# A SwiGLU feed-forward on one core: the head of the kernel, with half of the first row block transposed by DMA and its gate computed slice by slice of D

## The chip, the core and the metric

The kernel runs on one core of a Trainium2 chip. The core has a matrix engine (TensorE, PE in the profile, with its weight loads listed apart as PEld), VectorE (DVE), ScalarE (ACT), GpSimd (POOL) and SyncE (SP), which here only issues DMAs. Matmuls read SBUF and write PSUM. DMAs move data between HBM and SBUF; one kind (DMA_TRANSPOSE, the crossbar copy) transposes on its way. The metric is the device time of the whole program in microseconds, the median of several runs, with one launch. A profile is one execution; its span runs from the first instruction to the last.

## The reference

With x of 2048 rows and D = 640 columns and F = 1536 features, all in bf16:

```python
B, S, D, F = 1, 2048, 640, 1536

def reference(x, w_gate, w_up, w_down):
    g = _silu(x @ w_gate)
    u = x @ w_up
    return (g * u) @ w_down
```

## The kernel before

**Tiling.** Rows are cut into four blocks of 512 (`S_BLK`), D into five slices of 128 (`KD`, index `kd`), F into twelve chunks of 128 (`KF`, index `fc`). For each row block and each feature chunk, `proj` runs five matmuls (one for each slice of D) into a PSUM tile `pg` (gate), and five into `pu` (up). A weight block 128x128 is the stationary operand, and the transposed x, `xT`, is the moving one, with 512 columns, one for each row of x. `gate` then has ScalarE compute silu(pg) into SBUF (`sg`) and VectorE multiply it with `pu` into `aT`, in bf16. When a row block has its twelve chunks, the down projection multiplies `aT` with `w_down`: columns 512 to 639 of the output first, transposed (`po_t`), then four times 128 rows by 512 columns (`po_a`). The last four rows of x have their gate and up values from dot products on VectorE (`row_dots`), in gaps of its work; that part isn't touched.

**How x becomes xT.** Two ways are used. TensorE transposes a 128x128 block by a matmul with the identity (`transpose_chunk`, tile `pt` in PSUM), and ScalarE or VectorE copies the result into `xT`; this serves the first row block, whose x lies in `x_sb`. The other three row blocks come through `turn_x`, a crossbar copy by DMA issued on SyncE's queue: that of block 1 behind the weight loads, those of blocks 2 and 3 after the first row block.

**The head.** The first row block starts while its data is still arriving. `load_x` brings chunks of 128 rows: 0, 1 and 3 on SyncE, 2 on ScalarE. The weights come in pieces that grow (`W_CHUNKS`: feature chunks 0; 1; 2-3; 4-7; 8-11, gate then up); the first is split over both queues. `head()` writes TensorE's order out: 18 filler matmuls on a tile of ones (`warm`), which compute nothing that is used; the transposes of chunks 0 and 2, two fillers, those of chunk 1, two fillers; the projections of feature chunks 0 and 1 on rows 0 to 383; in between the transposes of chunk 3; then the remaining 128 rows. Feature chunks 2 to 11 follow in the loop at full width, in each of them five matmuls for gate and then five for up.

**What sets the order.** `keep_order` fixes the traced order on TensorE, ScalarE, VectorE and SyncE. ScalarE's queue holds its DMA issues, then the load of its function table and a first silu on one column (`silu_first`), then the copies of `xT`. Every DMA gets one of eight completion semaphores, in turn over both queues; a DMA whose semaphore is still in use by an earlier one waits on its issuing engine until that one has landed. In PSUM, gate and up tiles share the tag `gu` with four buffers, and the filler target `pw` takes one of them at the start; `po_a` and `po_b` have two each, and the transposes use them in the head.

Of the kernel before, what the change touches and what calls it, by code (L numbers as in the profile page):

```python
# [10 lines left out]
def _body(  # L11
# [8 lines left out]
    nc = tc.nc  # L20
    P = nc.NUM_PARTITIONS
    f32 = mybir.dt.float32
    bf16 = mybir.dt.bfloat16
    ACT = mybir.ActivationFunctionType
# [10 lines left out]
    S_BLK = 512  # L35
    NSB = S // S_BLK
    SUB = S_BLK // P
    DA = 512
    Q = 32
    N_WARM, N_GAP = 18, 2  # L40
    T = 4
    WT_STEP = 4
    ROW_J = 0
    W_CHUNKS = [(0, 1), (1, 2), (2, 4), (4, 8), (8, 12)]
    assert D % P == 0 and F % P == 0 and S % S_BLK == 0 and D > DA and SUB == 4

    consts = ctx.enter_context(tc.tile_pool(name="consts", bufs=1))
# [4 lines left out]
    )  # L52

    ident = consts.tile([P, P], bf16)
    x_sb = consts.tile([P, SUB, D], bf16)
    xT = consts.tile([P, KD, S], bf16)
    wg_sb = consts.tile([P, KD, F], bf16)
    wu_sb = consts.tile([P, KD, F], bf16)
# [18 lines left out]
    def wslice(a, b):  # L77
        return slice(a * P, b * P)

    def load_w(eng, dst, src, a, b):  # L80
        eng.dma_start(out=dst[:, :, wslice(a, b)], in_=src[:, :, wslice(a, b)])

    def load_x(eng, c0, c1):
        eng.dma_start(out=x_sb[:, c0:c1, :], in_=x_v[:, c0:c1, :])
# [14 lines left out]
        for a, b in zip(traced, traced[1:]):  # L99
            issue_order(a, b)  # L100

    ones = consts.tile([P, P], bf16)
    silu_first = consts.tile([P, 1], f32)
    nc.vector.memset(ones[:], 1.0)  # L104

    load_x(nc.sync, 0, 1)
    load_x(nc.scalar, 2, 3)
    load_x(nc.sync, 1, 2)
    for dst, src, k in ((wg_sb, wg_v, 3), (wu_sb, wu_v, 2)):
        for eng, k0, k1 in ((nc.scalar, 0, k), (nc.sync, k, KD)):  # L110
            eng.dma_start(out=dst[:, k0:k1, wslice(0, 1)], in_=src[:, k0:k1, wslice(0, 1)])
    load_w(nc.sync, wg_sb, wg_v, *W_CHUNKS[1])
    load_x(nc.sync, 3, 4)
    nc.scalar.activation(silu_first[:], ones[:, 0:1], ACT.Silu)
    load_w(nc.sync, wu_sb, wu_v, *W_CHUNKS[1])
    for a, b in W_CHUNKS[2:]:
        load_w(nc.sync, wg_sb, wg_v, a, b)
        load_w(nc.sync, wu_sb, wu_v, a, b)
    nc.sync.dma_start(out=wd_sb[:], in_=wd_v)
    wgt_v = w_gate.rearrange("d (kf p) -> d kf p", p=P)  # L120
    wut_v = w_up.rearrange("d (kf p) -> d kf p", p=P)

    def turn_x(sb):
        s_sl = slice(sb * S_BLK, (sb + 1) * S_BLK)
        nc.sync.dma_start_transpose(out=xT[:, :, s_sl], in_=xt_v[s_sl])

    def turn_w(dst, src):
        for a in range(0, KF, WT_STEP):
# [1 line left out]
                out=dst[:, a : a + WT_STEP, :], in_=src[:, a : a + WT_STEP, :]  # L130
            )

    turn_x(1)
    nc.sync.dma_start(
        out=x_row[:],
        in_=x2[S - T : S, :].rearrange("t d -> (t d)").partition_broadcast(P),
# [29 lines left out]
    def do_dots(n):  # L166
        for _ in range(n):
            next(dots, None)

    pw = psum.tile([P, S_BLK], f32, tag="gu", name="pw", bufs=4)  # L170

    def warm(n):
        for _ in range(n):
            nc.tensor.matmul(  # L174
                pw[:, 0:P], lhsT=ones[:], rhs=ones[:], start=True, stop=True
            )

    def transpose_chunk(c, parts):
# [8 lines left out]
                )  # L187
            copy(out=xT[:, k0:k1, c_sl], in_=pt[:])  # L188

    def proj(ps, w_sb, fc, sb, c0, c1, cols=lambda ap: ap):  # L190
        for kd in range(KD):
            nc.tensor.matmul(  # L192
                cols(ps[:, c0:c1]),
                lhsT=w_sb[:, kd, fc * P : (fc + 1) * P],
                rhs=cols(xT[:, kd, sb * S_BLK + c0 : sb * S_BLK + c1]),
                start=(kd == 0),
                stop=(kd == KD - 1),
            )

    def outer_chunks(ap):  # L200
        return ap.rearrange("p (c r) -> p c r", r=P)[:, 0:3:2]

    def gu_tiles():
        pg = psum.tile([P, S_BLK], f32, tag="gu", name="pg", bufs=4)
        pu = psum.tile([P, S_BLK], f32, tag="gu", name="pu", bufs=4)
        return pg, pu
# [8 lines left out]
        )  # L215

    def head():

        dve, act = nc.vector.tensor_copy, nc.scalar.copy
        split = [(act, "po_a", 0, 2), (dve, "po_b", 2, KD)]
        late = (SUB - 1) * P
        (pg0, pu0), (pg1, pu1) = gu_tiles(), gu_tiles()
        warm(N_WARM)
        transpose_chunk(0, [(dve, "po_a", 0, KD)])
        transpose_chunk(2, [(dve, "po_b", 0, KD)])
        warm(N_GAP)  # L230
        transpose_chunk(1, split)
        warm(N_GAP)
        proj(pg0, wg_sb, 0, 0, 0, late, outer_chunks)
        proj(pg0, wg_sb, 0, 0, P, 2 * P)
        proj(pu0, wu_sb, 0, 0, 0, late)
        proj(pg1, wg_sb, 1, 0, 0, late)
        transpose_chunk(3, split)
        proj(pu1, wu_sb, 1, 0, 0, late)
        for fc, pg, pu in ((0, pg0, pu0), (1, pg1, pu1)):
            proj(pg, wg_sb, fc, 0, late, S_BLK)  # L240
            proj(pu, wu_sb, fc, 0, late, S_BLK)
            gate(pg, pu, 0, fc, S_BLK)
        keep_order(mybir.EngineType.PE)
        keep_order(mybir.EngineType.Activation)

    head()
    for sb in range(NSB):
        n_s = S_BLK if sb < NSB - 1 else S_BLK - T
        for fc in range(KF):
            if sb == 0 and fc < 2:  # L250
                continue
            pg, pu = gu_tiles()
            proj(pg, wg_sb, fc, sb, 0, n_s)
            proj(pu, wu_sb, fc, sb, 0, n_s)
            gate(pg, pu, sb, fc, n_s)
            if sb > 0 and fc < KF - 2:
                do_dots(2)
# [51 lines left out]
                    row_tail()  # L309
                eng.dma_start(out=out2[s0 : s0 + P, c0:c1], in_=ot[:])  # L310
        if sb == 0:
            turn_x(2)
            turn_w(wuT, wut_v)
            turn_x(3)
    keep_order(mybir.EngineType.DVE)
    keep_order(mybir.EngineType.SP)

# [104 lines left out]
```

## Time and profile before

| what | value |
|---|---|
| time, median of 3 runs | 163.86 us (163.79 to 163.90) |
| the profiled execution's own time (its span) | 162.06 us |
| TensorE busy | 159.1 us, 98% of the span, 799 matmuls |
| VectorE / ScalarE busy | 111.7 / 42.8 us |
| gate and up matmuls, busy | 59.5 / 59.9 us |
| down projection matmuls, busy | 42.5 + 10.3 us |
| HBM read / written | 7.21 / 2.62 MB |

The span leaves out what lies around the first and the last instruction; it is 1.8 us under the median time. In the timeline a row is a run of like instructions: start, length, engine, line, operation, output and inputs, count, and in brackets the idle time before it and what ended it. "SPq" and "ACTq" rows are the issues of DMAs on SyncE and ScalarE; the length of an issue is the time that the engine spends on it, and "to landing" is counted from the start of the issue until the data has arrived. Busy times of matmuls are unions of overlapping instructions, so the pace of a stretch is read from the distance between starts.

### The profile page before, as it was taken

Reading aid. Unit: us, or ns where it says so; the run is one execution under the profiler, and the core shown is the slowest. Engines: PE = TensorE matmul, PEld = TensorE weight load, DVE = VectorE, ACT = ScalarE, POOL = GpSimd, SP = SyncE. Lnnn points to the kernel's source line nnn. Section 1 sums busy time; section 2 is a strip of 40 time slices with the busy share of each in tenths; the row PEclk is TensorE's granted clock in tenths of the full one; section 3 lists DMA queues with packets and bytes.
Section 4 is the critical chain, followed back from the end, with each engine's and each line's share of the span. In section 5 each row is a group of like instructions: output and inputs, shape, how many; then the busy total and the mean of one; then the engine's idle time right before and its main releaser. Section 6 shows DMA issues by size and latency. Waiting matters only on the chain.

```text
span 162.1 us, 2137 instructions
## 1 busy us (share of the span) xinstructions
PE 159.1 (98%) x799; PEld 77.5 (48%) x811; DVE 111.7 (69%) x251; ACT 42.8 (26%) x74; POOL 0.6 (0%) x6
## 2 busy tenths in 40 slices
PE   9999999999999999999999999999999999999995
PEld 8754444444444444444444444444444444445454
DVE  2242223599469999979919999979964999993000
ACT  3142222112222222221222322221214222222121
POOL 1000000000000000000000000000000000000000
DMA  7999999999089990003110000000320000000312
GB/s 211 252 316 366 360 210 263 230 229 94 32 191 177 241 226 12 0 0 34 65 65 0 4 0 2 0 0 3 62 69 32 0 0 0 0 4 0 51 38 73
DMA packets 42729, 15.86 MB, mean 98 GB/s; under 512 B 34528, under 2 KB 42592, under 8 KB 42720
## 3 DMA queue, kind: packets, MB, share of 16 engines
q1 hardware_dynamic: 33824, 14.88, 37.0%
q10 hardware_dynamic: 8896, 0.85, 5.5%
q8 instruction: 6, 0.10, 0.3%
q14 instruction: 3, 0.02, 0.0%
HBM read 7.21 MB, written 2.62 MB: 61 GB/s over the span
## 4 chain that ended last, share of the span: by engine, by line
PE 98%; issue 1%; DVE 0%
PE pu L192 32%; PE pg L192 32%; PE po_a L292 26%; PE po_t L263 6%; PE pw L174 1%; PE pt L183 1%; DVE ot_b L304 0%; DVE ones L104 0%
## 5 line engine op out<-in xcount | busy, mean ns | idle before, releaser
L192 PE MATMUL pg<-xT,wg_sb 128*128 128x512 bf16 (+4 forms) x248 | 59.5, 366 | 0.4
L192 PE MATMUL pu<-xT,wu_sb 128*128 128x512 bf16 (+3 forms) x250 | 59.9, 370 | 0.0
L213 DVE TENSOR_TENSOR aT<-sg,pu 128x512 bf16<-128x512 f32 (+1 forms) x48 | 32.7, 683 | 29.3 <-PE pu L192 27.9
L212 ACT ACTIVATE sg<-pg 128x512 f32<-128x512 f32 (+1 forms) x48 | 28.6, 596 | 67.4 <-PE pg L192 64.3
L292 PE MATMUL po_a<-wd_sb,aT 128*128 128x512 bf16 (+2 forms) x212 | 42.5, 358 | 0.2
L145 DVE SCALAR_TENSOR_TENSOR prod<-wgT,x_row 128x640 f32<-128x640 bf16 x48 | 39.4, 821 | 1.1
L145 DVE SCALAR_TENSOR_TENSOR prod<-wuT,x_row 128x640 f32<-128x640 bf16 x48 | 39.4, 821 | 1.0
L192 PEld LDWEIGHTS <-wg_sb 128*128 128x128 bf16 x255 | 24.3, 98 | 27.5 <-DMA wg_sb<-in_w_gate_dram 0.3
L192 PEld LDWEIGHTS <-wu_sb 128*128 128x128 bf16 x250 | 24.0, 98 | 27.5 <-DMA wu_sb<-in_w_up_dram 0.2
L292 PEld LDWEIGHTS <-aT 128*128 128x128 bf16 x216 | 20.7, 98 | 21.7 <-issue 0.2
L301 ACT CAST ot<-po_a 128x512 bf16<-128x512 f32 (+1 forms) x17 | 9.5, 561 | 32.1 <-PE po_a L292 19.9
L263 PE MATMUL po_t<-aT,wd_sb 128*128 128x512 bf16 (+1 forms) x47 | 10.3, 365 | 0.1
L263 PEld LDWEIGHTS <-wd_sb 128*128 128x128 bf16 x48 | 4.7, 98 | 5.1
L304 DVE CAST ot_b<-po_a 128x128 bf16<-128x128 f32 x1 | 0.3, 291 | 9.9 <-PE po_a L292 9.9
L188 DVE COPY xT<-pt 128x640 bf16<-128x640 bf16 (+1 forms) x4 | 1.7, 424 | 5.5 <-PE pt L183 5.5
L272 ACT CAST ot_t<-po_t 128x512 bf16<-128x512 f32 (+1 forms) x4 | 2.2, 559 | 11.6 <-PE po_t L263 11.6
L145 DVE DVE_READ_ACCUMULATOR prod<-wuT,x_row 128x1 f32 x48 | 3.9, 82 | 0.0
L145 DVE DVE_READ_ACCUMULATOR prod<-wgT,x_row 128x1 f32 x48 | 3.9, 81 | 0.0
L274 DVE STREAM_TRANSPOSE ot_q<-ot_t 128x512 bf16<-128x512 bf16 (+1 forms) x4 | 2.7, 676 | 1.7 <-ACT ot_t L272 1.7
L174 PE MATMUL pw<-ones 128*128 128x128 bf16 x22 | 2.8, 304 | 0.4 <-DVE ones L104 0.4
L174 PEld LDWEIGHTS <-ones 128*128 128x128 bf16 x22 | 2.3, 143 | 0.4 <-DVE ones L104 0.4
L183 PE MATMUL pt<-ident,x_sb 128*128 128x128 bf16 x20 | 2.2, 270 | 0.0
(13 smaller groups left out, 5.5 us busy)
## 6 DMA issues: line engine op xcount, KB each, us to landing
wd_sb<-in_w_down_dram SPq DMA_DIRECT2D x1, 1920.0 KB, 13.9
out_dram<-ot SPq DMA_DIRECT2D x15, 128.0 KB, 1.7
wg_sb<-in_w_gate_dram SPq DMA_DIRECT2D x2, 640.0 KB, 7.7
wu_sb<-in_w_up_dram SPq DMA_DIRECT2D x2, 640.0 KB, 8.6
x_row<-in_x_dram SPq DMA_DIRECT2D x1, 640.0 KB, 4.7
x_sb<-in_x_dram SPq DMA_DIRECT2D x3, 160.0 KB, 3.0
out_dram<-ot_q ACTq DMA_DIRECT2D x12, 32.0 KB, 1.9
wg_sb<-in_w_gate_dram SPq DMA_DIRECT2D x1, 320.0 KB, 4.8
```

Of the source, the lines that this page charges most:

```text
L145: nc.vector.scalar_tensor_tensor(out=prod[:], in0=wT[:, fc, :], scalar=1.0, in1=x_row[:, t, :], op0=ALU.mult, op1=ALU.mult, accum_out=acc[ ...
L174: nc.tensor.matmul(pw[:, 0:P], lhsT=ones[:], rhs=ones[:], start=True, stop=True)
L183: nc.tensor.transpose(out=pt[:, kd - k0, :], in_=x_sb[:, c, kd * P : (kd + 1) * P], identity=ident[:],)
L188: copy(out=xT[:, k0:k1, c_sl], in_=pt[:])
L192: nc.tensor.matmul(cols(ps[:, c0:c1]), lhsT=w_sb[:, kd, fc * P : (fc + 1) * P], rhs=cols(xT[:, kd, sb * S_BLK + c0 : sb * S_BLK + c1]), st ...
L212: nc.scalar.activation(sg[:, 0:n_s], pg[:, 0:n_s], ACT.Silu)
L213: nc.vector.tensor_tensor(out=aT[:, fc, s0 : s0 + n_s], in0=sg[:, 0:n_s], in1=pu[:, 0:n_s], op=ALU.mult)
L263: nc.tensor.matmul(po_t[:], lhsT=wd_sb[:, kf, DA:D], rhs=aT[:, kf, sb * S_BLK : sb * S_BLK + n_t], start=(kf == 0), stop=(kf == KF - 1),)
L272: nc.scalar.copy(ot_t[:], po_t[:])
L274: nc.vector.transpose(out=ot_q[:], in_=ot_t[:])
L292: nc.tensor.matmul(po[:], lhsT=aT[:, kf, s0 : s0 + P], rhs=wd_sb[:, kf, c0:c1], start=(kf == 0), stop=(kf == KF - 1),)
L301: nc.scalar.copy(ot[:], po[:])
```

## The change

The first row block is made from two halves. Rows 0-255 still come into `x_sb` and are transposed by TensorE, but each chunk of 128 rows is now loaded by columns: columns 0-255 on SyncE, 256-639 on ScalarE, which are also the two parts of its copy into `xT`. Rows 256-511 come by a crossbar copy, straight into `xT`. The gate weights of feature chunks 0-3 come as five slices of D, alternating between the queues; the up weights of these chunks follow behind the crossbar copy in two pieces.

`head()` holds four gate tiles at once (`EARLY`), goes over the slices of D in the outer loop and over the four feature chunks in the inner one, for rows 0-255 first (slice 0 in two steps of 128 rows) and for rows 256-511 then. After that come the up projections of the four chunks at full width, in the tiles `po_a` and `po_b`. The fillers are 16, all at the start, and both of their operands are one column of ones read 128 times over.

The moves on the queues: ScalarE issues four DMAs ahead of its table load (two pieces of x, gate slices 1 and 3) where it issued three; SyncE issues two pieces of x, gate slices 0, 2 and 4, the crossbar copy, and then the up weights.

```diff
--- before.py
+++ after.py
@@ -35,13 +35,15 @@
     S_BLK = 512
     NSB = S // S_BLK
     SUB = S_BLK // P
+    HALF = S_BLK // 2
     DA = 512
     Q = 32
-    N_WARM, N_GAP = 18, 2
+    N_WARM = 16
     T = 4
     WT_STEP = 4
     ROW_J = 0
-    W_CHUNKS = [(0, 1), (1, 2), (2, 4), (4, 8), (8, 12)]
+    EARLY = 4
+    W_CHUNKS = [(4, 8), (8, 12)]
     assert D % P == 0 and F % P == 0 and S % S_BLK == 0 and D > DA and SUB == 4
 
     consts = ctx.enter_context(tc.tile_pool(name="consts", bufs=1))
@@ -52,7 +54,7 @@
     )
 
     ident = consts.tile([P, P], bf16)
-    x_sb = consts.tile([P, SUB, D], bf16)
+    x_sb = consts.tile([P, HALF // P, D], bf16)
     xT = consts.tile([P, KD, S], bf16)
     wg_sb = consts.tile([P, KD, F], bf16)
     wu_sb = consts.tile([P, KD, F], bf16)
@@ -99,38 +101,40 @@
         for a, b in zip(traced, traced[1:]):
             issue_order(a, b)
 
-    ones = consts.tile([P, P], bf16)
+    def turn_x(r0, r1):
+        nc.sync.dma_start_transpose(out=xT[:, :, r0:r1], in_=xt_v[r0:r1])
+
+    ones = consts.tile([P, 1], bf16)
     silu_first = consts.tile([P, 1], f32)
     nc.vector.memset(ones[:], 1.0)
 
-    load_x(nc.sync, 0, 1)
-    load_x(nc.scalar, 2, 3)
-    load_x(nc.sync, 1, 2)
-    for dst, src, k in ((wg_sb, wg_v, 3), (wu_sb, wu_v, 2)):
-        for eng, k0, k1 in ((nc.scalar, 0, k), (nc.sync, k, KD)):
-            eng.dma_start(out=dst[:, k0:k1, wslice(0, 1)], in_=src[:, k0:k1, wslice(0, 1)])
-    load_w(nc.sync, wg_sb, wg_v, *W_CHUNKS[1])
-    load_x(nc.sync, 3, 4)
-    nc.scalar.activation(silu_first[:], ones[:, 0:1], ACT.Silu)
-    load_w(nc.sync, wu_sb, wu_v, *W_CHUNKS[1])
-    for a, b in W_CHUNKS[2:]:
+    for c in range(HALF // P):
+        for eng, k0, k1 in ((nc.sync, 0, 2), (nc.scalar, 2, KD)):
+            d_sl = slice(k0 * P, k1 * P)
+            eng.dma_start(out=x_sb[:, c, d_sl], in_=x_v[:, c, d_sl])
+    for kd in range(KD):
+        eng = (nc.sync, nc.scalar)[kd % 2]
+        eng.dma_start(
+            out=wg_sb[:, kd, wslice(0, EARLY)], in_=wg_v[:, kd, wslice(0, EARLY)]
+        )
+    turn_x(HALF, S_BLK)
+    nc.scalar.activation(silu_first[:], ones[:], ACT.Silu)
+    for a in range(0, EARLY, 2):
+        load_w(nc.sync, wu_sb, wu_v, a, a + 2)
+    for a, b in W_CHUNKS:
         load_w(nc.sync, wg_sb, wg_v, a, b)
         load_w(nc.sync, wu_sb, wu_v, a, b)
     nc.sync.dma_start(out=wd_sb[:], in_=wd_v)
     wgt_v = w_gate.rearrange("d (kf p) -> d kf p", p=P)
     wut_v = w_up.rearrange("d (kf p) -> d kf p", p=P)
 
-    def turn_x(sb):
-        s_sl = slice(sb * S_BLK, (sb + 1) * S_BLK)
-        nc.sync.dma_start_transpose(out=xT[:, :, s_sl], in_=xt_v[s_sl])
-
     def turn_w(dst, src):
         for a in range(0, KF, WT_STEP):
             nc.sync.dma_start_transpose(
                 out=dst[:, a : a + WT_STEP, :], in_=src[:, a : a + WT_STEP, :]
             )
 
-    turn_x(1)
+    turn_x(S_BLK, 2 * S_BLK)
     nc.sync.dma_start(
         out=x_row[:],
         in_=x2[S - T : S, :].rearrange("t d -> (t d)").partition_broadcast(P),
@@ -167,12 +171,13 @@
         for _ in range(n):
             next(dots, None)
 
+    ones_v = ones[:].to_broadcast([P, P])
     pw = psum.tile([P, S_BLK], f32, tag="gu", name="pw", bufs=4)
 
     def warm(n):
         for _ in range(n):
             nc.tensor.matmul(
-                pw[:, 0:P], lhsT=ones[:], rhs=ones[:], start=True, stop=True
+                pw[:, 0:P], lhsT=ones_v, rhs=ones_v, start=True, stop=True
             )
 
     def transpose_chunk(c, parts):
@@ -187,18 +192,18 @@
                 )
             copy(out=xT[:, k0:k1, c_sl], in_=pt[:])
 
-    def proj(ps, w_sb, fc, sb, c0, c1, cols=lambda ap: ap):
+    def proj_step(ps, w_sb, fc, sb, c0, c1, kd):
+        nc.tensor.matmul(
+            ps[:, c0:c1],
+            lhsT=w_sb[:, kd, fc * P : (fc + 1) * P],
+            rhs=xT[:, kd, sb * S_BLK + c0 : sb * S_BLK + c1],
+            start=(kd == 0 and c0 in (0, HALF)),
+            stop=(kd == KD - 1),
+        )
+
+    def proj(ps, w_sb, fc, sb, c0, c1):
         for kd in range(KD):
-            nc.tensor.matmul(
-                cols(ps[:, c0:c1]),
-                lhsT=w_sb[:, kd, fc * P : (fc + 1) * P],
-                rhs=cols(xT[:, kd, sb * S_BLK + c0 : sb * S_BLK + c1]),
-                start=(kd == 0),
-                stop=(kd == KD - 1),
-            )
-
-    def outer_chunks(ap):
-        return ap.rearrange("p (c r) -> p c r", r=P)[:, 0:3:2]
+            proj_step(ps, w_sb, fc, sb, c0, c1, kd)
 
     def gu_tiles():
         pg = psum.tile([P, S_BLK], f32, tag="gu", name="pg", bufs=4)
@@ -215,31 +220,27 @@
         )
 
     def head():
-
-
-
-
-
         dve, act = nc.vector.tensor_copy, nc.scalar.copy
         split = [(act, "po_a", 0, 2), (dve, "po_b", 2, KD)]
-        late = (SUB - 1) * P
-        (pg0, pu0), (pg1, pu1) = gu_tiles(), gu_tiles()
+        pgs = [
+            psum.tile([P, S_BLK], f32, tag="gu", name="pg", bufs=4)
+            for _ in range(EARLY)
+        ]
         warm(N_WARM)
-        transpose_chunk(0, [(dve, "po_a", 0, KD)])
-        transpose_chunk(2, [(dve, "po_b", 0, KD)])
-        warm(N_GAP)
-        transpose_chunk(1, split)
-        warm(N_GAP)
-        proj(pg0, wg_sb, 0, 0, 0, late, outer_chunks)
-        proj(pg0, wg_sb, 0, 0, P, 2 * P)
-        proj(pu0, wu_sb, 0, 0, 0, late)
-        proj(pg1, wg_sb, 1, 0, 0, late)
-        transpose_chunk(3, split)
-        proj(pu1, wu_sb, 1, 0, 0, late)
-        for fc, pg, pu in ((0, pg0, pu0), (1, pg1, pu1)):
-            proj(pg, wg_sb, fc, 0, late, S_BLK)
-            proj(pu, wu_sb, fc, 0, late, S_BLK)
-            gate(pg, pu, 0, fc, S_BLK)
+        for c in range(HALF // P):
+            transpose_chunk(c, split)
+
+        steps = [(0, 0, P), (0, P, HALF)]
+        steps += [(kd, 0, HALF) for kd in range(1, KD)]
+        steps += [(kd, HALF, S_BLK) for kd in range(KD)]
+        for kd, c0, c1 in steps:
+            for fc in range(EARLY):
+                proj_step(pgs[fc], wg_sb, fc, 0, c0, c1, kd)
+
+        for fc in range(EARLY):
+            pu = psum.tile([P, S_BLK], f32, tag=("po_a", "po_b")[fc % 2], name="pu")
+            proj(pu, wu_sb, fc, 0, 0, S_BLK)
+            gate(pgs[fc], pu, 0, fc, S_BLK)
         keep_order(mybir.EngineType.PE)
         keep_order(mybir.EngineType.Activation)
 
@@ -247,7 +248,7 @@
     for sb in range(NSB):
         n_s = S_BLK if sb < NSB - 1 else S_BLK - T
         for fc in range(KF):
-            if sb == 0 and fc < 2:
+            if sb == 0 and fc < EARLY:
                 continue
             pg, pu = gu_tiles()
             proj(pg, wg_sb, fc, sb, 0, n_s)
@@ -309,9 +310,9 @@
                     row_tail()
                 eng.dma_start(out=out2[s0 : s0 + P, c0:c1], in_=ot[:])
         if sb == 0:
-            turn_x(2)
+            turn_x(2 * S_BLK, 3 * S_BLK)
             turn_w(wuT, wut_v)
-            turn_x(3)
+            turn_x(3 * S_BLK, 4 * S_BLK)
     keep_order(mybir.EngineType.DVE)
     keep_order(mybir.EngineType.SP)
```

## The prediction

> **What bounds the kernel now.** I read the page's span, busy times and chain first, then TensorE's timeline over the first 14 us, then the ScalarE and SyncE timelines over the same stretch, and last the rows of the crossbar copies (DMA_TRANSPOSE).
>
> ```profile
> span 162.1 us, 2137 instructions
> ...
> PE 159.1 (98%) x799; PEld 77.5 (48%) x811; DVE 111.7 (69%) x251; ACT 42.8 (26%) x74; POOL 0.6 (0%) x6
> ...
> PE 98%; issue 1%; DVE 0%
> ```
>
> TensorE is the chain. So a change is worth what it takes from TensorE's instructions, its waits, or the stretch in which it runs slowly. The diff changes only the head, so I compare when the gate of feature chunk 4 of the first row block starts; behind that the programs are the same.
>
> ```profile
> 0.40 2.10 PE L174 MATMUL pw<-ones 128*128 128x128 bf16 x18 [0.40 <-DVE ones L104]
> 2.39 1.25 PE L183 MATMUL pt<-ident,x_sb 128*128 128x128 bf16 x10
> 3.43 0.42 PE L174 MATMUL pw<-ones 128*128 128x128 bf16 x2
> ...
> 4.22 0.98 PE L192 MATMUL pg<-xT,wg_sb 128*128 128x256 bf16 x10
> 5.04 0.98 PE L192 MATMUL pu<-xT,wu_sb 128*128 128x384 bf16 x5
> ...
> 8.94 1.24 PE L192 MATMUL pg<-xT,wg_sb 128*128 128x512 bf16 x4
> 10.02 1.24 PE L192 MATMUL pu<-xT,wu_sb 128*128 128x512 bf16 x5
> ...
> 13.26 1.24 PE L192 MATMUL pg<-xT,wg_sb 128*128 128x512 bf16 x5
> ```
>
> Projections begin at 4.22; chunk 4 begins at 13.26. Ten 128-column transposes from 2.39 to 3.43 are 0.104 us apart (0.107 once they run); the five from 6.72 to 7.00 are 0.056 apart, the same instruction at double speed. Single starts put the switch at 3.8, which is 3.4 us after the first filler. (The clock column says 1.00 throughout, so I go by spacing.) A 512-column matmul takes 0.216 (five in 1.08).
>
> ```profile
> 0.12 0.41 ACTq L84 DMA_DIRECT2D x_sb<-in_x_dram  x1
> 0.56 0.45 ACTq L111 DMA_DIRECT2D wg_sb<-in_w_gate_dram  x1
> 1.04 0.51 ACTq L111 DMA_DIRECT2D wu_sb<-in_w_up_dram  x1
> 1.58 1.28 ACT L114 ACT_TABLE_LOAD   x1 [1.58 <-issue]
> 2.88 0.20 ACT L114 ACTIVATE silu_first<-ones 128x1 f32<-128x1 bf16 x1
> 4.03 0.37 ACT L188 COPY xT<-pt 128x256 bf16<-128x256 bf16 x1 [0.95 <-PE pt L183]
> ```
>
> ScalarE has three DMA issues, a table load and a first silu ahead of its first copy, ready at 3.08, and still waits 0.95 us for TensorE.
>
> ```profile
> 1.90 0.49 SPq L81 DMA_DIRECT2D wg_sb<-in_w_gate_dram  x1
> 2.73 0.34 SPq L84 DMA_DIRECT2D x_sb<-in_x_dram  x1
> ...
> 9.72 1.80 SPq L119 DMA_DIRECT2D wd_sb<-in_w_down_dram  x1
> 11.56 12.26 SPq L125 DMA_TRANSPOSE xT<-in_x_dram  x1
> ...
> 44.76 2.49 SPq L125 DMA_TRANSPOSE xT<-in_x_dram  x1
> ```
>
> ```profile
> DMA to landing us min/median/max: 4.9/5.2/14.3
> ```
>
> The last line is for the three crossbar copies of 512 rows. DMAs take eight semaphores in turn, so the ninth waits for the landing of the first on its semaphore: SyncE stands still from 2.39 to 2.73, the landing of ScalarE's x transfer (0.12 + 2.6). The crossbar copy issued into an idle queue took 2.49 to issue and 4.9 to land; the one behind wd held SyncE 12.26, until 0.2 after wd landed (9.72 + 13.9 = 23.6), and landed 2.0 after its own issue ended.
>
> **Fillers.** 18 + 2 + 2 become 16, reading one column with step 0. The memset of 128x128 took 0.17; for 128x1 the nearest row is GpSimd's 0.10, so fillers start near 0.33 and end near 0.33 + 16 x 0.107 = 2.04. No row shows a step-0 operand: at best 0.107 each as now, at worst weight load and matmul in series, 0.15 + 0.107, ending at 4.4. I take 0.107, since the operand has the same shape.
>
> **x rows 0-255.** Chunk 0 comes as 64 KB on SyncE and 96 KB on ScalarE; 160 KB landed at 2.34 (SyncE) and 2.72 (ScalarE). Smaller pieces land no later: I take 2.0 and 2.45, chunk 1 about 2.75. The ten transposes, still 0.107 apart, run with small gaps from 2.1 to 3.3. Ten others with two VectorE copies go; the fillers between them go too.
>
> **ScalarE is next.** It now issues four DMAs: starts were 0.44 to 0.54 apart, so the table load moves from 1.58 to about 1.94 (bounds 1.88 to 2.1), the first silu ends at 3.44, and the two copies of xT columns 0-255 end at 3.81 and 4.20. The cover of 0.95 is gone: TensorE waits for them from 3.3. VectorE's two copies (0.36 each) end by 4.0, hidden.
>
> **Gate by slices.** Copy to dependent matmul was 0.07 (VectorE's second copy ended 4.15, matmul 4.22). So gate starts at 3.88, earlier by 0.34. Slice 0 on chunk 0: 4 x 0.056, to 4.10; then a wait for the second ScalarE copy, to 4.27; 4 x 0.056, to 4.49; slices 1 to 4 on 256 columns at 0.1085: 16 of them, to 6.23; the other half, 20 x 0.1085 = 2.17, to 8.40; the up projections, 20 x 0.2157 = 4.31, to 12.71. Against 13.26 that is 0.55 less, if no wait comes in. The projections' columns are the same in both. Gone are the five transposes at 6.72 (0.28) and some 0.05 of waits.
>
> **Gate slices by DMA.** 128 KB each, due at 3.88, 4.49, 4.93, 5.36 and 5.80. SyncE's third DMA landed at 0.91 + 3.3 = 4.2 when it was cut into 256 B rows; these have 1 KB rows, and as many bytes (512 KB) had come for x by about 3.4. I take 3.3 to 4.6 for the five: hidden, by 0.5 or more.
>
> **Crossbar copy, rows 256-511.** Due at 6.23. SyncE issues x, x, slice 0, slice 2, then slice 4, which waits for ScalarE's first x piece (about 2.45), then the crossbar copy at 2.9. Half of 512 rows saves half of the 2.49 of issue, so it lands 4.9 - 1.25 = 3.65 later, at 6.55. By the copy that had loads ahead: issue ends at 4.15 to 4.8 (0.2 after slice 4 lands), landing 2.0 later, 6.15 to 6.8. I take 6.4: a wait of 0.17. Bounds: 0 and, by the row of 14.3 us and wgT's 6.9 (less 1.25: landing at 8.55), 2.3.
>
> **Queued behind it.** SyncE's up loads wait for that issue: chunks 0-1 go at 4.2 to 4.8, move behind the crossbar packets and land near 7.6 (5.3 to landing was the row for 320 KB before, so 10.1 is the worst), due at 8.40; chunks 2-3 near 9.0, due 10.56. Gate chunks 4-7 landed at 5.08 + 6.6 = 11.7, due 13.26, up chunks 4-7 at 6.15 + 7.5 = 13.7, due 14.34. The bytes ahead are the same 3.2 MB, with half as many 256 B rows; due times now are 12.9 and 14.0, so covers are 0.6 or more. PSUM: four gate tiles take all of that tag, the fourth in the fillers' bank, free at 2.1; up tiles use the transposes' banks, free by 4.2. ScalarE and VectorE (0.60 and 0.69 a tile) run beside 1.08 of TensorE. All at nothing.
>
> **Sum.** -0.55 + 0.17 = -0.38 us. The profiled span of 162.06 stands 1.8 below the median of 163.86, which I leave as it is: 163.48, say 163.5. Single differences under 0.2% (0.33 us) can't be told from no change, so this is just over it.
>
> **Rivals.** *The clock turns a window late.* Ahead of the switch TensorE was busy for 97% of 3.4 us. Now it has 16 + 10 instructions of 0.107, 2.78 of 3.41 (81%), and stands still just before 3.75. If that isn't enough and the next chance is 3.4 later, at 7.15, matmuls between 3.88 and 7.15 run at half speed: 1.63 lost, less the two waits of 0.17 that vanish in it: chunk 4 at 12.88 + 1.63 - 0.34 = 14.17, which is 0.91 later than now, 164.8. For it: the removed fillers lie in that stretch. Against: the present idle before 2.39 didn't delay the switch. This is my case on the other side; it decides as soon as 81% is too little. [...]
>
> *The crossbar copy is late.* Each us past 6.23 is a us. At 6.8 it eats the gain (163.9); at 7.2 it is 164.3; at 8.55 it is 165.6. For it: the copies issued with transfers under way held their issue until those landed. Against: less than 300 KB lies ahead.
>
> *The step-0 fillers are slow.* At 0.15 each they end at 2.7, the transposes at 3.8, and the ScalarE copies stay where they are (163.5); at 0.257 they end at 4.4, the transposes and the first copy follow, and the gate begins near 5.0, 164.6.
>
> **Chances.** Forecast (crossbar wait 0 to 0.4) 0.47; crossbar later 0.26; clock late 0.20; fillers slow or an up load late 0.07. Of the forecast's 0.47, waits under 0.2 (0.33) are faster by over 0.2%, the rest (0.14) within; of the late copies 0.10 within (landing up to 7.1), 0.16 slower; of the last 0.03 within, 0.04 slower. Faster 0.33, within 0.27, slower 0.40. The likeliest case's own range is 163.3 to 163.7. The whole range is 163.25 to 164.9: it takes in the late clock and a copy late by up to 1.6, and leaves out the worst.
>
> **What would show it.** TensorE's timeline: gate's first matmul at 3.9, waiting for ScalarE; 256-column matmuls 0.11 apart from 4.5 (0.21 is the late clock); a wait at about 6.2 for xT of under 0.4; chunk 4 at 12.9. The crossbar copy issued near 2.9, landed near 6.4. Fillers 0.107 apart. I would be wrong by a wait for wu_sb near 8.4, or by ScalarE's table load beyond 2.1.

## The result, and the profile after

The changed kernel takes 165.16 us (median of 22 executions, 163.63 to 166.35); the kernel before takes 163.88 beside it (22, 163.44 to 164.64). The ratio over the single executions is 1.0059, with a 95% interval of 1.0038 to 1.0079, and that of the two medians 1.0078: slower by 0.6 to 0.8%. The profiled execution took 165.17 us for a span of 163.77.

Three lines of the page (head, busy times, releasers of the chain):

```profile
span 163.8 us, 2100 instructions
...
PE 159.9 (98%) x782; PEld 77.6 (47%) x794; DVE 110.8 (68%) x249; ACT 42.4 (26%) x74; POOL 0.6 (0%) x6
...
PE 96%; DMA 2%; SPq 0%; issue 0%; DVE 0%
```

TensorE has 17 instructions fewer and is busy 0.8 us longer, and a DMA now has 2% of the chain. Both can be seen in TensorE's timeline of the first 16 us:

```profile
0.31 1.89 PE L179 MATMUL pw<-ones 128*128 128x128 bf16 x16 [0.31 <-DVE ones L109]
2.14 0.97 PE L188 MATMUL pt<-ident,x_sb 128*128 128x128 bf16 x7
3.35 0.50 PE L188 MATMUL pt<-ident,x_sb 128*128 128x128 bf16 x3 [0.23 <-DMA x_sb<-in_x_dram]
4.65 6.23 PE L196 MATMUL pg<-xT,wg_sb 128*128 128x128 bf16 x44 [0.81 <-DMA wg_sb<-in_w_gate_dram]
10.72 4.48 PE L196 MATMUL pu<-xT,wu_sb 128*128 128x512 bf16 x19
15.04 1.24 PE L196 MATMUL pg<-xT,wg_sb 128*128 128x512 bf16 x5
```

The gate starts at 4.65 instead of 4.22, after a wait of 0.81 for the first gate slice (the last transpose started at 3.54, so at its pace of 0.107 TensorE stood still for 1.0). Its 44 matmuls take 6.1 us to the first of the up projections, at 10.72. Chunk 4 begins at 15.04 instead of 13.26: 1.78 us later, and the span is longer by 1.72. So the whole loss between these two profiles is in the head.

Why the 44 take so long is seen in the groups of instructions by shape. First the stretch from 5.5 to 8.0, then that from 8.3 to 10.6 (the numbers behind the bar are busy us and mean ns):

```profile
L196 PE MATMUL pg<-xT,wg_sb 128*128 128x256 bf16 x12 | 2.8, 417 | 0.0
...
L196 PE MATMUL pg<-xT,wg_sb 128*128 128x256 bf16 x23 | 2.7, 275 | 0.0
```

The same instruction: 12 in 2.5 us, and then 23 in 2.3 us. By single starts they are 0.213 apart up to 8.04, and 0.109 from 8.21 on; the one between takes 0.166, so the pace doubles within it, at 8.15. I call that moment the clock's switch. In the profile before it was at 3.80, by the same working. (The clock column says 1.00 for every stretch. But six of the traces hold a record of when the full clock was granted, and in each it begins within 0.05 us of the switch by starts: here at 8.15.)

The queues, first ScalarE and then SyncE in the timeline:

```profile
0.12 0.88 ACTq L114 DMA_DIRECT2D x_sb<-in_x_dram  x2
1.03 0.94 ACTq L117 DMA_DIRECT2D wg_sb<-in_w_gate_dram  x2
2.00 1.28 ACT L121 ACT_TABLE_LOAD   x1 [2.00 <-issue]
3.29 0.20 ACT L121 ACTIVATE silu_first<-ones 128x1 f32<-128x1 bf16 x1
3.40 0.63 ACT L193 COPY xT<-pt 128x256 bf16<-128x256 bf16 x2
```

```profile
0.00 0.87 SPq L114 DMA_DIRECT2D x_sb<-in_x_dram  x2
0.91 1.77 SPq L117 DMA_DIRECT2D wg_sb<-in_w_gate_dram  x3
2.72 2.33 SPq L105 DMA_TRANSPOSE xT<-in_x_dram  x1
5.10 1.15 SPq L83 DMA_DIRECT2D wu_sb<-in_w_up_dram  x2
```

ScalarE has finished both copies by 4.03, 0.6 before the gate. Of the DMAs, the page of the first 2.3 us gives the median time to landing of the first two slices on SyncE, and the page from 2.6 to 5 us that of the crossbar copy:

```profile
wg_sb<-in_w_gate_dram SPq DMA_DIRECT2D x2, 128.0 KB, 3.8
...
xT<-in_x_dram SPq DMA_TRANSPOSE x1, 4.5
```

Slice 0, issued at 0.91, landed at 4.61. A landing is told by 16 updates of a semaphore, which I read as one for each of the 16 DMA engines: 13 of them had come by 3.68; the last three took until 4.18, 4.26 and 4.61. The crossbar copy, issued at 2.72, landed at 7.26; no wait comes of that here, since the second half of the gate began only at about 8.5.

From these rows one sum describes every kernel that keeps the slices. Behind the start of the gate lie 8.67 us of work at the full clock (44 gate matmuls 2 x 4 x 0.056 + 36 x 0.1085, and 20 up matmuls x 0.2157). Every us between the start of the gate and the switch adds half a us, since it does half the work. Waits come on top: here 4.65 + 8.67 + (8.15 - 4.65)/2 = 15.07, against the measured 15.04.

### The profile page after: what moved, and what is told of

The parts are those of the page before. It is cut to its first block, busy times and chain, and to the rows that moved or that the text cites. A ratio compares the mean times of both kernels' runs of the same rounds, so it can differ in the third digit from the quotient of the medians.

```text
span 163.8 us, 2100 instructions
## 1 busy us (share of the span) xinstructions
PE 159.9 (98%) x782; PEld 77.6 (47%) x794; DVE 110.8 (68%) x249; ACT 42.4 (26%) x74; POOL 0.6 (0%) x6
## 3 DMA queue, kind: packets, MB, share of 16 engines
q1 hardware_dynamic: 33440, 14.75, 36.9%
## 4 chain that ended last, share of the span: by engine, by line
PE 96%; DMA 2%; SPq 0%; issue 0%; DVE 0%
PE pg L196 33%; PE pu L196 32%; PE po_a L293 26%; PE po_t L264 6%; DMA wg_sb<-in_w_gate_dram 2%; SPq L114 0%; DVE ot_b L305 0%
## 5 line engine op out<-in xcount | busy, mean ns | idle before, releaser
L196 PE MATMUL pg<-xT,wg_sb 128*128 128x512 bf16 (+3 forms) x258 | 60.5, 369 | 1.1 <-DMA wg_sb<-in_w_gate_dram 0.8
L196 PE MATMUL pu<-xT,wu_sb 128*128 128x512 bf16 (+1 forms) x239 | 59.0, 379 | 0.1
L196 PEld LDWEIGHTS <-wg_sb 128*128 128x128 bf16 x264 | 26.4, 102 | 28.0 <-DMA wg_sb<-in_w_gate_dram 1.1
L196 PEld LDWEIGHTS <-wu_sb 128*128 128x128 bf16 x240 | 23.5, 98 | 28.0
L193 DVE COPY xT<-pt 128x384 bf16<-128x384 bf16 x2 | 0.7, 357 | 3.3 <-PE pt L188 3.3
L179 PE MATMUL pw<-ones 128*128 128x128 bf16 x16 | 1.9, 313 | 0.3 <-DVE ones L109 0.3
L179 PEld LDWEIGHTS <-ones 128*128 128x128 bf16 x16 | 1.6, 147 | 0.3 <-DVE ones L109 0.3
```

The costliest lines, as they stand in the source:

```text
L179: nc.tensor.matmul(pw[:, 0:P], lhsT=ones_v, rhs=ones_v, start=True, stop=True)
L196: nc.tensor.matmul(ps[:, c0:c1], lhsT=w_sb[:, kd, fc * P : (fc + 1) * P], rhs=xT[:, kd, sb * S_BLK + c0 : sb * S_BLK + c1], start=(kd == 0 ...
```

## The experiments

**The theory after the result**: two things, the first slice late and the clock switching late because TensorE was kept too little busy. The rivals: the crossbar copy itself costs it (its packets or its hold on the queue), or the slices do.

**The changed kernel again**, nothing edited.

> The changed kernel once more, for a second trace. If the switch follows a grid of time that the program doesn't set, it comes at another time than 8.04, with the time following it by half the difference (between 163.6 and 166.4). If three DMA engines lagging behind with gate slice 0 (thirteen of sixteen had it by 3.7, the last at 4.6) is a property of this order of loads, slice 0 lands at 4.4 to 4.8 again; if it was chance, at 3.7 to 4.0.

It took 165.93 us, span 164.54, and its TensorE timeline has

```profile
4.78 6.85 PE L196 MATMUL pg<-xT,wg_sb 128*128 128x128 bf16 x44 [1.16 <-DMA wg_sb<-in_w_gate_dram]
...
15.78 1.24 PE L196 MATMUL pg<-xT,wg_sb 128*128 128x512 bf16 x5
```

The slice is late again (4.73), and the switch, by starts, is at 9.55, 1.40 later than in the first profile. Chunk 4 is 0.74 later and the span 0.76; the sum has 15.83 (4.78 + 8.67 + 4.77/2), of which 0.70 comes from the switch and 0.07 from the gate, which starts 0.13 later. So the moment of the switch isn't fixed by the program, and it alone moves the time by 0.7 us between two executions.

**TensorE kept busy.** Two fillers between the two parts of each chunk's transposes, and ten behind the last:

```diff
-            transpose_chunk(c, split)
+            transpose_chunk(c, split[:1])
+            warm(2)
+            transpose_chunk(c, split[1:])
+            warm((0, 10)[c])
```

> The changed kernel with fillers in TensorE's idle stretches: 2 between the two parts of each chunk's transposes and 10 behind the last, ahead of the gate. Data order as in the changed kernel. Theory A (the loss is a late clock, because TensorE stood idle ahead of the gate): the switch comes between 3.7 and 6 us after the span's start instead of 8.04; the first gate matmul stays at about 4.65 because slice 0 lands at 4.6; with the clock up, chunk 4 starts at about 13.8 and the median is 163.9 to 164.4, 0.8 to 1.3 under the changed kernel. Rival B (the loss is late data alone): the median stays within 0.2 of 165.2. Rival C (fillers on one column don't count for the clock): the switch stays near 8, median 165.2. Under A about 0.5 us over the kernel before remains, which is the late gate slices and the crossbar copy (landed 7.26, due at about 6.85 with a fast clock).

164.48 us (163.97 to 165.35), just above the range that theory A gave; ratio to before 1.0029, interval 1.0012 to 1.0046. Of its timeline:

```profile
3.57 0.89 PE L179 MATMUL pw<-ones 128*128 128x128 bf16 x10
4.61 4.76 PE L196 MATMUL pg<-xT,wg_sb 128*128 128x128 bf16 x44 [0.15 <-DMA wg_sb<-in_w_gate_dram]
9.20 4.48 PE L196 MATMUL pu<-xT,wu_sb 128*128 128x512 bf16 x20
13.52 1.24 PE L196 MATMUL pg<-xT,wg_sb 128*128 128x512 bf16 x5
15.38 0.82 PE L196 MATMUL pu<-xT,wu_sb 128*128 128x512 bf16 x3 [0.62 <-ACT sg L217]
```

The slice is as late as before, the gate starts as late (4.61), but the switch is at 3.87 and chunk 4 at 13.52 instead of 15.04. Now the crossbar copy shows: between the two halves of the gate there is a gap from 6.71 to 7.02, about 0.21 more than the spacing. 4.61 + 8.67 + 0.21 = 13.49. (In the last row a wait has come in, in chunk 4; the page puts it down to `sg`, but the up weights of chunks 4 to 7 had only landed at 15.34, since one DMA engine of the 16 was late.)

> e1 once more, beside e10 and for a second trace. The first trace of e1 had a wait of 0.8 us for the up weights of chunks 4-7 (landed at 15.34). If that is part of this order of loads, it comes again; if one DMA engine lagged by chance, those weights land near 13.9 as in the changed kernel and the wait is gone, with chunk 4 at 13.4 to 13.8 where the switch is early.

The same kernel on another chip: 164.41 (163.65 to 164.67), ratio 1.0024 (1.0008 to 1.0041), against 164.12. Switch 4.34, gate 4.81, crossbar wait 0.25, and

```profile
13.79 1.03 PE L196 MATMUL pg<-xT,wg_sb 128*128 128x512 bf16 x4
```

near what the sum has (4.81 + 8.67 + 0.25 = 13.73). The up weights had landed at 14.08 and nothing waited: that wait was no part of the change. So the fillers take about half of the loss away (0.59% to 0.27%; the intervals of the two kernels overlap a little, the switches in the traces do not: 3.87 and 4.34 against 8.15 and 9.55). In these two traces nothing is lost to the clock behind the gate, and what remains is the late gate: chunk 4 starts 0.26 and 0.53 later than in the profile before. That the other half of the medians' difference is the late gate too is argued from this: no trace shows a slower execution of this kernel, and the one with chunk 4 at 13.79 took 164.09, less than its median.

**The crossbar copy taken out.** The kernel with more fillers, rows 256-511 by two plain loads in the crossbar copy's place, and ten TensorE transposes with their copies ahead of the second half:

```diff
-    turn_x(HALF, S_BLK)
+    load_x(nc.sync, 2, 3)
+    load_x(nc.sync, 3, 4)
...
-        for kd, c0, c1 in steps:
+        for n, (kd, c0, c1) in enumerate(steps):
+            if n == KD + 1:
+                for c in range(HALF // P, SUB):
+                    transpose_chunk(c, split)
```

> As e1, but rows 256-511 come as two plain loads on SyncE at the crossbar copy's place and are transposed by TensorE, ten transposes more (10 x 0.056 = 0.56 us). If the crossbar copy is a loss (it holds its engine for 2.33 us and lands at 7.26), this is faster than e1: the up loads go 1.5 us earlier and the wait of about 0.4 at the second half of the gate goes. If the crossbar copy costs little, this is slower than e1 by 0.15 to 0.6. By theory A I expect 0.1 to 0.2 slower than e1.

164.91 (164.58 to 166.87), ratio 1.006 (1.0037 to 1.0084); the kernel with fillers and the crossbar copy had 164.48 on the same chip. Its timeline:

```profile
4.73 2.68 PE L197 MATMUL pg<-xT,wg_sb 128*128 128x128 bf16 x24
7.25 0.72 PE L189 MATMUL pt<-ident,x_sb 128*128 128x128 bf16 x10
8.26 2.34 PE L197 MATMUL pg<-xT,wg_sb 128*128 128x256 bf16 x20 [0.29 <-ACT xT L194]
```

The gate starts no earlier (4.73) without the crossbar copy, so that copy isn't what delays the slice. From 7.25 to 8.26 go one us for the transposes and the wait for their copies, where the crossbar copy cost 0.2 to 0.25. So beside these transposes it is a gain, not the loss. (Chunk 4 starts 1.24 later here than with the crossbar copy, at 14.76; 0.36 of that is a later switch, at 5.44.)

**The slices taken out.** Weights by feature chunk as before, two of them early; crossbar copy kept, the up weights of chunk 1 behind it:

```diff
-    EARLY = 4
-    W_CHUNKS = [(4, 8), (8, 12)]
+    EARLY = 2
+    W_CHUNKS = [(2, 4), (4, 8), (8, 12)]
...
+    for dst, src, k in ((wg_sb, wg_v, 3), (wu_sb, wu_v, 2)):
+        for eng, k0, k1 in ((nc.scalar, 0, k), (nc.sync, k, KD)):
+            eng.dma_start(out=dst[:, k0:k1, wslice(0, 1)], in_=src[:, k0:k1, wslice(0, 1)])
+    load_w(nc.sync, wg_sb, wg_v, 1, 2)
     turn_x(HALF, S_BLK)
...
+    load_w(nc.sync, wu_sb, wu_v, 1, 2)
...
+        for c0, c1 in ((0, HALF), (HALF, S_BLK)):
+            for fc, pg, pu in ((0, pg0, pu0), (1, pg1, pu1)):
+                proj(pg, wg_sb, fc, 0, c0, c1)
+                proj(pu, wu_sb, fc, 0, c0, c1)
...
```

> Undoes the slices alone: x rows 0-255 by columns and the crossbar copy of rows 256-511 stay as in the changed kernel, but gate and up weights come by feature chunk as in the kernel before (chunk 0 split over the queues, chunk 1's gate ahead of the crossbar copy, its up behind it), two chunks are computed on rows 0-255 and then on rows 256-511, and there are fillers in the gaps (2, 2 and 5) as in e1. Theory (what is left of the loss once the clock is kept is the late slices of 128 KB): the first gate matmul comes at 4.1 to 4.4 and the median falls by 0.2 to 0.5 under e1, to about the kernel before. Rival (the crossbar copy is what is late): TensorE has only 2.2 us of work from rows 0-255, waits for the copy from about 6.4 to 7.0, and the median equals e1's or is up to 0.4 over it.

165.59 (164.78 to 166.0), ratio 1.0096 (1.0064 to 1.0128): about 1.1 over the kernel with fillers, which neither the theory nor the rival had. The gate starts at 4.31, earlier than with slices, but

```profile
6.05 0.71 PE L194 MATMUL pg<-xT,wg_sb 128*128 128x256 bf16 x5
8.22 0.72 PE L194 MATMUL pu<-xT,wu_sb 128*128 128x256 bf16 x5 [1.46 <-DMA wu_sb<-in_w_up_dram]
```

and in SyncE's queue

```profile
2.64 1.52 SPq L105 DMA_TRANSPOSE xT<-in_x_dram  x1
4.21 0.57 SPq L83 DMA_DIRECT2D wu_sb<-in_w_up_dram  x1
```

The load that is queued behind the crossbar copy is issued at 4.21 and lands at 8.17. With slices, TensorE has gate work for four chunks by then and doesn't need it. So taking the slices out, in this order of loads, loses more than the earlier gate gains; the switch, at 5.67, costs 0.68 of it by the half rule, and the wait is 1.46. An order with chunk 1's up weights ahead of the crossbar copy wasn't run, so the price of the slices alone stays open.

**Slice 0 earlier.** Three orders of the first loads, each in the kernel with more fillers. First, slice 0 second on SyncE, ahead of its piece of x chunk 1:

```diff
...
+    load_cols(nc.sync, 0, 0, 2)
+    load_cols(nc.scalar, 0, 2, KD)
+    load_slice(nc.sync, 0)
+    load_cols(nc.scalar, 1, 2, KD)
+    load_cols(nc.sync, 1, 0, 2)
+    for kd in range(1, KD):
+        load_slice((nc.sync, nc.scalar)[kd % 2], kd)
...
```

> As e1 (fillers in the gaps), with one swap on SyncE: gate slice 0 is issued second, at 0.46, and columns 0-255 of x chunk 1 third, at 0.91. Theory (slice 0 is late because of what is issued and flows ahead of it): it lands near 4.0 instead of 4.6, the first gate matmul moves to 4.0 to 4.2, and the median falls by 0.2 to 0.5 under e1, near the kernel before. Rival (the engines lag because weights are read for the first time, whatever lies ahead): slice 0 still lands at 4.5 to 4.7 on its last engines, the median equals e1 within 0.15.

165.82 (165.45 to 167.23), ratio 1.0122 (1.0088 to 1.0156). Slice 0 landed at 2.94, 1.7 earlier. But the piece of x that took its place in the queue landed at 4.35 (13 of its engines by 3.30, the 15th at 4.23):

```profile
4.39 0.40 PE L195 MATMUL pt<-ident,x_sb 128*128 128x128 bf16 x2 [1.42 <-DMA x_sb<-in_x_dram]
...
6.18 3.08 PE L203 MATMUL pg<-xT,wg_sb 128*128 128x128 bf16 x23
```

Second, all of x chunk 1 on ScalarE, and all slices on SyncE:

```diff
...
+    load_cols(nc.sync, 0, 0, 2)
+    load_cols(nc.scalar, 0, 2, KD)
+    load_slice(nc.sync, 0)
+    load_cols(nc.scalar, 1, 0, KD)
+    for kd in range(1, KD):
+        load_slice(nc.sync, kd)
...
```

> As e1, with ScalarE issuing only two DMAs (columns 256-639 of x chunk 0, then the whole of chunk 1) and SyncE x columns 0-255 of chunk 0, then gate slices 0 to 4 in a row, then the crossbar copy at about 2.75. ScalarE's first copy can begin at about 2.6 instead of 3.4. If slice 0 then lands near 3.7 to 4.0, the gate begins there, chunk 4 starts at 12.9 to 13.2 and the median is 0.3 to 0.8 under e1, which would be equal to the kernel before or up to 0.3 better. If slices are late whatever the queue, the gate still begins at 4.5 or later and the median equals e1 within 0.15.

165.6 (164.14 to 166.23), ratio 1.0096 (1.0061 to 1.013). Slice 0 at 3.50, x chunk 1 at 3.69; TensorE waits 0.79 for the latter, the ten fillers run after that, and the gate starts at 5.52. In both traces the switch is late as well (7.90 and 9.36). Third, slice 0 in two halves of 64 KB, one on each queue:

```diff
+    for eng, kd, a, b in (
+        (nc.sync, 0, 0, 2),
+        (nc.scalar, 0, 2, EARLY),
+        (nc.sync, 1, 0, EARLY),
+        (nc.scalar, 2, 0, EARLY),
+        (nc.sync, 3, 0, EARLY),
+        (nc.sync, 4, 0, EARLY),
+    ):
...
```

> As e1, but gate slice 0 comes as two halves of 64 KB, one on each queue, ahead of slices 1 to 4; the number of ScalarE's issues stays four. If slice 0 is late because its queue's engines share their time with slice 1, it lands near 4.2 instead of 4.6, the gate begins at about 4.3 and the median falls by 0.1 to 0.35 under e1. If the engines lag at that time whatever lies in the queues, it lands at 4.5 again and the median equals e1 within 0.15.

164.68 (163.97 to 165.27), ratio 1.0033 (1.0015 to 1.0051), against 164.41 of the kernel without the split on the same chip: no better. The halves landed at 4.17 and 4.34, and the gate started right behind the fillers, but SyncE now issues one DMA more ahead of the crossbar copy, which went out at 3.21 and landed at 7.85:

```profile
4.58 2.47 PE L200 MATMUL pg<-xT,wg_sb 128*128 128x128 bf16 x24
7.89 2.34 PE L200 MATMUL pg<-xT,wg_sb 128*128 128x256 bf16 x20 [0.84 <-DMA xT<-in_x_dram]
...
14.49 1.24 PE L200 MATMUL pg<-xT,wg_sb 128*128 128x512 bf16 x5
```

What follows from the three: it wasn't that the slice is a weight, or large, or read with 1 KB rows, since second on SyncE it landed at 2.94 and 3.50. Moving it forward puts something else where it was: the piece of x landed at 4.35, the half slice at 4.17. But the third place on SyncE isn't a rule either: with all slices there the third DMA landed at 3.93, and it was the fourth that took until 4.69.

**What the clock's switch is worth, and what counts for it.** The kernel before without fillers:

```diff
-    N_WARM, N_GAP = 18, 2
+    N_WARM, N_GAP = 0, 0
```

> The kernel before without its 22 fillers, nothing else. Theory A: TensorE's first work is the transposes at 2.39, so the switch comes between 5.8 and 9.2; matmuls between 4.2 and the switch run at half speed, 0.8 to 2.5 us lost, less the waits for weights that vanish in it; median 164.6 to 165.4, with a spread of over 1 us between executions. Rival B (the clock is not what the fillers buy, the data sets the pace): 163.9, and the switch still near 3.8.

164.86 (164.82 to 164.97), ratio 1.005 (1.0035 to 1.0064). The gate starts at 4.16 and TensorE has no wait for data from there to chunk 4, as in before; the switch moves, to 7.42, which shows in two groups of the same five matmuls:

```profile
5.78 1.79 PE L192 MATMUL pu<-xT,wu_sb 128*128 128x384 bf16 x5
...
8.50 0.98 PE L192 MATMUL pu<-xT,wu_sb 128*128 128x384 bf16 x5
```

So the fillers are worth 0.8 us to this kernel by the medians. Between the two traces it is more: chunk 4 starts at 14.75 instead of 13.26, and half of 7.42 - 4.16 is 1.63. The spread that I had expected, over 1 us, isn't there: the five executions lie within 0.15 us, as if the switch had come at nearly the same moment in all of them.

> The kernel before once more, for a second trace. If the switch follows a grid of time that the program doesn't set, it comes at another time than 3.8 (between 3.4 and 6.8), and the span is longer than 162.06 by half of what lies between 4.2 and the switch. If the first filler sets it, the switch is at 3.8 again and the span within 0.2 of 162.06.

The kernel before, profiled again: 163.35 us, span 162.04, and a switch at 3.35 instead of 3.80, with the first filler at 0.39 against 0.40. So the switch isn't a fixed time behind the first filler, as I had read it. Both switches lie ahead of the gate and slow none of its matmuls.

Last, the kernel before with 13 fillers at the start instead of 18, which are in one kernel transposes by the identity and in the other plain matmuls of the same shape, also with the identity. Until the gate starts, at about 4.4, TensorE has nothing but transposes in the first:

```diff
...
-            nc.tensor.matmul(
-                pw[:, 0:P], lhsT=ones[:], rhs=ones[:], start=True, stop=True
-            )
+            nc.tensor.transpose(out=pw[:, 0:P], in_=ones[:], identity=ident[:])
```

> The kernel before with 13 + 2 + 2 fillers that are transposes by the identity (which is ready near 0.95, so TensorE's work begins there). If transposes don't count for the clock, nothing counts before 4.2, the switch comes at 6.5 or later, and the time is 0.7 to 1.5 over e6_matmul_fillers. If they count as other matmuls do, switch (between 4.3 and 7.5) and median equal those of e6_matmul_fillers within 0.3.

> The kernel before with 13 + 2 + 2 fillers that are plain matmuls of ones with the identity as the moving operand, which also begin near 0.95. The switch comes between 4.3 and 7.5, and the median is 0.1 to 0.4 over the kernel before, for 0.55 us less of early work. It is the comparison for e6_turn_fillers.

164.64 (163.95 to 165.21, ratio 1.0037, interval 1.0018 to 1.0056) and 164.58 (163.71 to 164.96, 1.0028, 1.0007 to 1.005): no difference between them. (Both medians are 0.7 over the kernel before, where I had expected 0.1 to 0.4 for the matmuls.) In the profiled execution of the matmuls the switch came at 5.41 and the time was 163.92. In that of the transposes the switch came at 7.05 and the time was 164.80; eight of the ten were below that, the lowest by 0.85. By half a us for each us, their switches came earlier than 7.05, by up to 1.7, though no trace shows these. If transposes didn't count, little but the work from 4.48 on could, and even half of the 3.4 us that lie between the first filler and the switch in the profile before (0.40 to 3.80) would put the switch at 6.2 or later, by my estimate; by the half rule two of the ten (163.95 and 164.16) switched well before that. So the medians and these two speak for transposes that count for the clock much as matmuls do; no trace by itself shows it.

## Why the prediction was wrong

I forecast 163.5 us and a gain; 165.16 lies above the range. Two steps failed. One is that of the gate slices by DMA: "I take 3.3 to 4.6 for the five: hidden, by 0.5 or more". The first, taken at 3.3 and due at 3.88, landed at 4.61 and 4.73 in the two traces. The other is the clock, which the sum put at nothing; the half speed up to 8.15 cost 1.75, more than the late slice. The rest, by the steps of the prediction:

- **Fillers, x, ScalarE: right, but for the last piece of x.** One column read 128 times cost nothing: the fillers run 0.107 apart, as in the kernel before. The pieces of x landed at 2.10, 2.33, 2.67 and 3.30 (forecast 2.0, 2.45, and 2.75 for the last); the 0.55 of the last was hidden. The table load is at 2.00, within its bounds, and the copies end at 4.03 for 4.20. The gate could have started at about 3.9 as forecast, but for the slice.
- **Gate slices: wrong.** They landed at 4.61, 4.79, 5.25, 5.42 and 5.94. I had a row that said 4.2 for the third DMA on SyncE and took it as too high, for longer rows and as many bytes (those that had come for x by 3.42 were 480 KB, not 512). Thirteen of the engines were done by 3.68, ahead of the due time; the last three decided. Even the row of 4.2 would have been 0.4 too low. Price: 0.77 at the gate.
- **The clock: the rival to which I gave 0.20.** Its price of 164.8 was for a switch at 7.15 and a gate at 3.88. With the measured 8.15 and 4.65 the same working gives chunk 4 at 15.06, from 12.88: 0.77 for the gate, 1.75 for the clock, less the two waits of 0.17. The span by that is 162.06 - 0.38 + 2.18 = 163.86, and 163.77 was measured. So the size holds, and of the mechanism the half speed until a later switch; the chance was too small. What doesn't hold is a switch at a fixed time behind the first filler (3.35 against 3.80, with the first filler at 0.39 and 0.40). No run shows the next chance 3.4 later either: that was my estimate from one distance in the profile before (0.40 to 3.80), and the changed kernel switched at 8.15 and 9.55, which is 4.35 and 5.75 behind 3.80. The 81% was a count of matmuls at 0.107; by that count the stretch of 3.41 that ended in the switch of the second set with more fillers (4.34) had 80%, so a switch has come with less than 81%. The changed kernel's stretch from 1.33 to 4.74, with the wait for the slice in it, had 50%.
- **The crossbar copy: nearly right.** Issued at 2.72 (forecast 2.9); the issue held SyncE for 2.33 instead of 1.25 to 1.9, and it landed at 7.26 instead of 6.4, inside the bounds. Under the slow clock no one waited; with the clock early it costs 0.2 to 0.25, against the 0.17 in the sum, because the gate starts later too.
- **Queued behind it: no wait, as forecast.** The up weights landed at 9.10 and 10.18 (forecast 7.6 and 9.0), and were due at 10.7 and 12.9 by the slow clock. With the clock early these two have landed in time too.
- **The gain itself: there, but small.** In the two traces of the kernel with more fillers, where the clock is early, 8.91 and 8.98 us lie between the start of the gate and chunk 4, against 9.04 before. With the gate 0.4 to 0.6 late, that isn't enough.
- **The base.** I read the span of 162.06 as 1.8 below "the median" and left it so. Span and time of one execution differ by 1.31 to 1.43 in the traced runs (165.17 - 163.77 = 1.40; 163.35 - 162.04 = 1.31 for the kernel before), so that profile was of an execution of about 163.4, as fast as the fastest of the 22 (163.44). Its switch, 3.80, lay ahead of the gate, and so part of what I compared with was luck.

How busy TensorE was ahead of a switch can be read with the view of windows. Its columns are the stretch, its length, TensorE's busy time and count, the clock column, the DMA share and GB/s. The length of 3.41 is that from the first filler's weight load to the switch in the profile before (0.39 to 3.80). Of the changed kernel, the two stretches of 3.41 us that end 3.41 before its switch and at it:

```profile
1.33:4.74 3.41, 2.37 (x21) 1.00 0.88 265
4.74:8.15 3.41, 3.41 (x21) 1.00 0.98 194
```

Of the kernel with more fillers, in its second set, and then of the one with all slices on SyncE:

```profile
0.93:4.34 3.41, 3.02 (x29) 1.00 0.85 249
```

```profile
2.54:5.95 3.41, 2.62 (x26) 1.00 0.99 267
```

In all 14 traces TensorE was busy for 87% or more of the 3.41 us that end in the switch (2.96, the least, in the kernel before profiled again). Six traces hold a whole stretch of this length ahead of that one; there it was busy for 78% or less (2.66, the most, in the kernel with transposes as fillers), and no switch came at its end. (Busy time in this view takes a matmul at its whole length; by the count at 0.107 the two are 80 and 73%.) That such a share sets the moment of the switch, and over which stretch it counts, no trace shows. The moment isn't the same in two executions of one program: the changed kernel switched at 8.15 and 9.55, and the one before at 3.80 and 3.35. Against that stand the five executions of the kernel without fillers, which lie within 0.15 us; that stays open. Here, where 0.2% is a result, the late clock is about half of the change's effect by the medians (0.59% against 0.27%).

By these shares the wait for the slice may have cost more than its 0.77, which is my estimate: with the gate at 3.88, the stretch 1.33 to 4.74 would have held 2.37 + 0.77 = 3.14 (92%), and with 87% a switch has come. No run shows it: none of my orders brought slice 0 and all of x in time, and the kernel with more fillers fills the gap of the slice and those that the change opened together. Nor is there a trace of one of the six fastest executions of the changed kernel. Its 22 times fall into six from 163.63 to 164.05 and sixteen from 164.75 to 166.35. In the first trace TensorE was busy for 3.16 of the 3.41 us from 0.29 to 3.70 (93%), ahead of the wait for the slice; that the six switched at about that time would fit their times, and it isn't shown.

No version of the changed head was faster than the kernel before.

## What to carry to other kernels

A load that is fed to the first matmul must be judged by its slowest DMA engine (here 13 were done at 3.68 and the last at 4.61): take the row of the trace for the same place in the queue as the least, and don't lower it for fewer bytes or longer rows (here the row had 4.2). At the start of this kernel idle time of TensorE cost twice, once as a wait (0.81 for the slice) and once by a late clock (a switch at 8.15 and 9.55, against 3.87 and 4.34 with more fillers); so fillers belong in each gap that a late load can open, not only at the start, and an edit that takes fillers out has to be priced with the loads at their latest. Before a single trace is taken as the base, set its own time (span and what lies around it, here 1.31 to 1.43) against the spread of the other executions: a fast one has a piece of luck in it that the change won't have.

## What the runs showed that I had not expected

- In five of the nine traces of the changed head and its variants, between 2 and 5 us, two to four of the 16 DMA engines lag by 0.8 to 1.2 us. In the changed kernel they carry slice 0 from 3.68 (13 engines) to 4.61; with slice 0 second they carry the piece of x from 3.30 to 4.35. In the other four the engines' ends spread more evenly, with gaps under 0.5. In the two traces of the kernel before none lags there: its third DMA on SyncE was done by its engines from 3.7 to 4.2. The cause stays open.
- The issue of a crossbar copy held the issuing engine, and by no simple measure of its size: 2.33 us for 256 rows behind the slices, 1.52 behind the weights by feature chunk, where 512 rows issued into an idle queue took 2.49. It did not wait for the last slice (the issue ended at 5.05, that slice landed at 5.94).
- The clock's switch differed by 1.40 us between two executions of the changed kernel (8.15 and 9.55) and by 0.45 between two of the kernel before (3.80 and 3.35), and by the half rule the first moves the time by half of that (0.70 of the 0.74 above). In a kernel of 164 us this is the same size as the effects under test, and much of the spread between executions may be that.
